# When a search step that waits for matmul products is due: a planned time worked out anew at each unit, instead of once and with a cap

## The chip, the cores and the metric

The kernel runs on one core of a Trainium2 chip. The metric is the device time of one execution in microseconds (us). The engines are TensorE (PE), VectorE (DVE), ScalarE (ACT), GpSimd (POOL, which issues the indirect DMAs) and SyncE (SP).

## The reference

Four batches of eight heads go through a retention layer (attention with a decay and no softmax); its output is a matrix `x` of 3072 tokens by 512. A mixture of eight experts follows. Tokens are given to experts greedily, the largest logit first, at most 384 tokens to an expert, and each token goes through its own expert alone:

```python
logits = x @ w_gate
order = np.argsort(-logits.flatten())
for idx in order:
    tok, e = (int(idx) // E, int(idx) % E)
    if assigned[tok] >= 0 or counts[e] >= cap:
        continue
    assigned[tok] = e
    counts[e] += 1
for e in range(E):
    mask = assigned == e
    h = np.maximum(x[mask] @ w1[e], 0.0)
    out[mask] = h @ w2[e]
```

## The kernel before

The first 100 us are the retention layer. After that PE works through eight experts in the order in which the greedy rule fills them. An expert is two blocks of matmuls: `mm1` (96 matmuls `ph`, 384 columns each, in eight groups of 12) and `mm2` (72 matmuls `py`, 512 columns each, three for each of eight slices in each of three row blocks). Each float32 operand is split into a high part, a rounded copy made by ACT (`w1h`, `w2h`, `xh`, `hh`), and a low part, a subtraction made by DVE (`w1l`, `w2l`, `xlo`, `hl`), so every product takes three matmuls.

Beside the experts runs a search. `search(n)` finds which expert is filled n-th and by which tokens, while PE multiplies for expert n-1. It has two rounds. In each, DVE compares the logits with 64 thresholds (`cmp`, two halves), PE counts (12 small matmuls `psm<-oh,cmp`, the products here), ACT negates one half of the counts (`ng`), DVE makes a flag of each (`sg`), and PE adds these up (`psm<-sg,onesb`, called the number below), which DVE reads (`nmb`). After the rounds PE ranks the tokens (`psm<-Wq,ub`), places them (`psm<-V,ob`), and turns places into token numbers (`psm<-pls,selq`, called the token step), which DVE reads (`own`, `idx`). A DVE tail follows that prepares the next search (`eo` to `a`, then `a`, `oh`, `th`, `cmp`, `off`, `qn`, `cmp`). From the token numbers POOL gathers the expert's rows (`xg`) and weights (`wraw`). The rows are transposed by PE in three blocks (`pt<-ident,xg`, into two buffers named `pt`), and ACT and DVE split each block into `xh` and `xlo`; a third block needs the buffer of the first, which is free when the first `xlo` is done.

Nothing here is ordered at run time: every engine runs its own queue in the order in which the program was written. That order comes from a planner, a clock kept in Python while the program is built. `mm1` and `mm2` yield after each unit of a few matmuls. Then `Beside.tick` moves the clock on and lets the search take its next step if the step's `due` time is past, and `Feed.tick` does the same for fetches, splits and transposes. Where a step reads products of PE, its due time comes from `hear()`: in the planner's picture, PE's signal is not heard while POOL is booked to issue an indirect DMA (1250 ns each, by `issue`), nor for 500 ns (`AFTER`) after it. `hear()` looks at the issues that are booked at that moment and returns at most 1200 ns (`DEAF`):

```python
if n:
    yield clk.pe + hear() + COPIED
full(pc, ng, sg)
```

Of the kernel before, what the change touches and what calls it, by code (L numbers as in the profile page):

```python
# [22 lines left out]
E = 8  # L23
# [6 lines left out]
READY, SWITCH, HEAR, COPIED = 200, 50, 200, 350  # L30
DEAF, AFTER, ISSUE = 1200, 500, 1250
# [27 lines left out]
READY0 = 0  # L59
# [5 lines left out]
def tile_retention_moe(ctx: ExitStack, tc: tile.TileContext, qkv, wg, w1, w2,  # L65
# [65 lines left out]
    class Clock:  # L131

        pe = dve = pool = dma = 0
        busy = []

    clk = Clock()

# [19 lines left out]
    def hear():  # L157

        t = clk.pe + HEAR
        clk.busy = [p for p in clk.busy if p[1] + AFTER > t]  # L160
        for p in clk.busy:
            if p[0] <= t:
                t = max(t, p[1] + AFTER)
        return min(DEAF, t - clk.pe)

    def issue(at):

        clk.pool = max(clk.pool, clk.pe, at) + ISSUE
        clk.busy.append((clk.pool - ISSUE, clk.pool))

    def pe_step(n):
        clk.pe += max(35, n / 2.4)
        clk.dve = max(clk.dve, clk.pe + hear())
# [6 lines left out]
    def tt(out_, a, b_, op):  # L180
        return ve.tensor_tensor(out_, a, b_, op=op)

    def bc(ap, n):
        return ap[:, :, None].to_broadcast([128, ap.shape[1], n])
# [27 lines left out]
    def reach(cols, k, m, cmp, th):  # L212
        nt = th.shape[1]
        tt(cmp[:, cols], bc(m[:, cols], nt), cb(th, nt, k), OP.is_ge)
# [10 lines left out]
    def full(pc, ng, sg):  # L225

        ve.scalar_tensor_tensor(sg[0:64], pc[0:64, 0:E], float(CAP), ng, op0=OP.subtract, op1=OP.is_ge)
# [428 lines left out]
    def ps_small(shape):  # L656
        return pp.tile(shape, F32, name=small[0], bufs=2 if small[0] == "pt" else 1)
# [15 lines left out]
    def count_pairs(cmp, oh, eng=None):  # L673
        pc = ps_small([128, 2 * E])
        for k in range(COLS // 2):
            by_two(pc, cmp, oh, 2 * k, k == 0, k == COLS // 2 - 1)
        return pc, other_half(pc, eng)
# [77 lines left out]
    def search(n):  # L755

        nonlocal un  # L760
        last = n == E - 1
        code = mp.tile([128, 1], F32, name="code", bufs=2)
        if last:
            ve.tensor_reduce(code, left.pop(n), axis=AX.X, op=OP.max)
            ve.tensor_copy(Wq[:, 0:COLS], un)
        else:
            m, a, oh, cmp = ready.pop(n)
            for i in range(2):
                sg = sgs[i]
                if n or i:  # L770
                    yield
                    pc, ng = count_pairs(cmp, oh, None if n > 1 else ve)
                    if n:
                        yield clk.pe + hear() + COPIED
                    full(pc, ng, sg)
                    yield
                num = ps_small([128, E])
                te.matmul(num, onesb, sg, start=True, stop=True)
                nm = sw.tile([128, 1], F32, name="nmb", bufs=2)
                ve.tensor_reduce(nm, num, axis=AX.X, op=OP.max)  # L780
                if not i:
                    th = sw.tile([128, 64], F32, name="th")
                    ve.scalar_tensor_tensor(th, nm.to_broadcast([128, 64]), near[:, 0:1], offn[n], op0=OP.mult,
                                            op1=OP.add)
                    cmp = sw.tile([128, COLS, 64], BF, name="cmp", bufs=2)
                    for h in range(2):
                        cc = slice(h * COLS // 2, (h + 1) * COLS // 2)
                        reach(cc, COLS // 2, m, cmp, th)
                        if not h and n:
                            yield  # L790
                    q = sw.tile([128, 1], F32, name="q", bufs=2)
                    ve.scalar_tensor_tensor(q, nm, near[:, 0:1], qn[n], op0=OP.mult, op1=OP.add)
                else:
                    eh = sw.tile([128, E], BF, name="eh")
                    ve.scalar_tensor_tensor(eh, num, nm, codet, op0=OP.is_equal, op1=OP.mult)
                    tv = sw.tile([128, 1], F32, name="tv", bufs=2)
                    ve.scalar_tensor_tensor(tv, nm, near[:, 1:2], q, op0=OP.mult, op1=OP.add)
                    ve.tensor_reduce(code, eh, axis=AX.X, op=OP.max)
            sel = sw.tile([128, COLS], BF, name="sel")
            ve.tensor_scalar(sel, a, code, None, op0=OP.is_equal)  # L800
            ve.scalar_tensor_tensor(Wq[:, 0:COLS], m, tv, sel, op0=OP.is_ge, op1=OP.mult)
        if n == 0:
            fill(FILL[0])
        ve.tensor_tensor_scan(Sc[:, 1:COLS + 1], Wq[:, 0:COLS], zer[:, 0:COLS], 0.0, op0=OP.add, op1=OP.add)
        wix = weight_rows(code, n)
        named[n] = wix.bitcast(U32), clk.dve
        if n == 0:
            fetch_w("w1", 0, 0, wix.bitcast(U32), raw0)
        if not last:
            both = sw.tile([128, 1], F32, name="both")  # L810
            ve.tensor_reduce(both, eh, axis=AX.X, op=OP.add)
            unf = un
            un = sw.tile([128, COLS], F32, name="un", bufs=2)
            tt(un, unf, Wq[:, 0:COLS], OP.subtract)
        yield
        rk = ps_small([128, COLS + 1])
        te.matmul(rk, ub, Wq, start=True, stop=False)
        te.matmul(rk, onesb, Sc[:, 0:COLS + 1], start=False, stop=True)
        s0 = sw.tile([128, COLS], I32, name="s0")
        ve.scalar_tensor_tensor(s0, rk[:, 0:COLS], 32.0, Wq[:, 0:COLS], op0=OP.add, op1=OP.mult)  # L820
        if not last:
            ve.scalar_tensor_tensor(bad, rk[:, COLS:], float(CAP), bad, op0=OP.not_equal, op1=OP.max)
        if n == 0:
            fill(FILL[1])
        V, low = high_slots(s0, 1, n, None if n else nc.scalar)
        ob = low_slots(low)
        if not last:
            ve.scalar_tensor_tensor(bad, both, code, bad, op0=OP.not_equal, op1=OP.max)
            alone(oh, unf if n else None)
        yield  # L830
        pls = places(V, ob, None if n else ve)
        yield clk.pe + hear() + COPIED if n else None
        idx = tokens_of_slots(pls)
        oix = mp.tile([128, KT], I32, name="oix", bufs=4)
        ve.scalar_tensor_tensor(oix, bad.to_broadcast([128, KT]), float(2 * N), idx, op0=OP.mult, op1=OP.add)
        found[n] = idx.bitcast(U32), wix.bitcast(U32), oix.bitcast(U32)
        known[n] = clk.dve
        yield
        if not last:
            left[n + 1] = close(n, code, left.pop(n))  # L840
            if n + 2 < E:
                m1, a1, oh1, cmp1 = ready[n + 1] = prep_tiles()
                best(Lw, allc, m1, oh1)()
                codes(allc, oh1, a1)
                if n:
                    yield
                tt(a1, a1, un, OP.mult)
                tt(oh1, oh1, bc(un, E), OP.mult)
                rest = below(n + 1, tv)
                th = next(rest)  # L850
                for h in range(2):
                    reach(slice(h * COLS // 2, (h + 1) * COLS // 2), COLS // 2, m1, cmp1, th)
                    if not h:
                        next(rest)
                    yield
# [247 lines left out]
    class Beside:  # L1103


        def __init__(self):
            self.gen, self.n, self.due = None, -1, 0
            self.held = lambda: False

        def step(self):  # L1110
            if self.gen is None:
                self.n += 1
                self.gen = search(self.n)
            clk.pe = max(clk.pe, self.due) + SWITCH
            due = None
            try:
                due = next(self.gen)
            except StopIteration:
                self.gen = None
            self.due = due or clk.dve + (READY if self.n else READY0)  # L1120

        def tick(self, ns, cur):
            clk.pe += ns
            while not self.held() and self.due <= clk.pe and (self.gen is not None or self.n + 1 <= min(cur + 2, E - 1)):
                self.step()

        def finish(self, n):
# [2 lines left out]

    clk.dve = clk.pe = clk.pool = clk.dma = 0
    clk.busy.clear()
    side = Beside()
    left_over[0] = lambda i: pp.tile([128, DM], F32, name="py" if i % 2 else "ph", bufs=2 if i % 2 else 3)
    for k in STEPS:
# [248 lines left out]
```

## Time and profile before

| | us |
|---|---|
| median of 3 runs | 401.94 (401.54 to 402.74) |
| the profiled execution, its own time | 404.41 |
| its span, first to last instruction | 402.7 |
| busy in the span: PE, DVE, ACT, POOL | 388.3, 272.0, 156.5, 146.9 |

The profiled execution has 1.7 us outside the span and is 2.5 us above the median of the runs. The granted clock of PE is 0.998 of full speed, so the clock is no matter here.

### The profile page before, as it was taken

The page shows a single profiled execution, that of the slowest core. Times are in us where ns is not written, and L with a number is a line of the kernel's source. Part 1 is how long each engine was busy: PE and PEld are TensorE (multiplying, and loading weights), DVE is VectorE, ACT ScalarE, POOL GpSimd, SP SyncE. Part 2 cuts the span into 40 slices and gives each one's busy share as a digit, 9 for nine tenths or more (in the row PEclk, how much of TensorE's full clock was granted, in tenths as well). Part 3 has the DMA queues.
Part 4 walks back from the last instruction along what each step waited for, and adds up shares of the span by engine and source line. Part 5 has one row for each costly group of instructions (what it writes and reads, how often), then busy time and mean ns, then how long its engine had stood idle before and what let it go on. Part 6 is the DMA issues. An engine that isn't in the chain of part 4 may idle for free.

```text
span 402.7 us, 8469 instructions
## 1 busy us (share of the span) xinstructions
PE 388.3 (96%) x3457; PEld 338.1 (84%) x3459; DVE 272.0 (68%) x640; ACT 156.5 (39%) x285; POOL 146.9 (36%) x162
## 2 busy tenths in 40 slices
PE   8899999997999999999989999999999999999994
PEld 6798999973798889879868997898789889989983
DVE  5349768968899589858848895896688157156400
ACT  1342424243471275147215533453453256156210
POOL 5488774202620620341261451352356128020011
PEclk9999999999999999999999999999999999999999
DMA  7999988888643572383375374177146405810001
GB/s 276 422 414 420 387 311 266 201 194 288 201 199 104 174 260 55 141 285 134 106 225 218 132 252 166 52 215 278 49 156 224 178 27 168 354 52 28 2 28 59
DMA packets 22824, 77.50 MB, mean 192 GB/s; under 512 B 2677, under 2 KB 11639, under 8 KB 16121
## 3 DMA queue, kind: packets, MB, share of 16 engines
q0 software_dynamic: 8448, 46.14, 32.7%
q1 hardware_dynamic: 14330, 30.74, 21.6%
q8 instruction: 29, 0.48, 0.5%
q14 instruction: 17, 0.14, 0.1%
HBM read 64.29 MB, written 12.58 MB: 191 GB/s over the span
## 4 chain that ended last, share of the span: by engine, by line
PE 64%; issue 13%; DVE 11%; DMA 5%; POOL 2%; ACT 2%; POOLq 1%; SPq 1%; another core or an unknown queue 0%; ACTq 0%; DVEq 0%
PE py L1092 24%; PE ph L1050 20%; PE yp L414 5%; PE sc L369 4%; DMA ld<-qkv 3%; PE pt L1000 2%; PE yp L399 2%; PE psm L154 2%; PE TP L429 2%; DVE w1l L154 2%; PE sc L501 2%; DVE cmp L154 1%; DVE w2l L154 1%; POOL wraw L954 1%; DVE am L372 1%
## 5 line engine op out<-in xcount | busy, mean ns | idle before, releaser
L1050 PE MATMUL ph<-xh,w1h 128*128 128x384 f32 x248 | 81.9, 343 | 0.1
L1050 PE MATMUL ph<-xlo,w1h 128*128 128x384 f32 x256 | 81.7, 336 | 0.2 <-DVE xlo L154 0.2
L1050 PE MATMUL ph<-xh,w1l 128*128 128x384 f32 x256 | 81.5, 335 | 0.0
L1092 PE MATMUL py<-w2h,hh 128*128 128x512 f32 x184 | 75.3, 409 | 0.0
L1092 PE MATMUL py<-w2l,hh 128*128 128x512 f32 x184 | 72.0, 392 | 0.0
L1092 PE MATMUL py<-w2h,hl 128*128 128x512 f32 x184 | 72.0, 392 | 0.0
L1073 POOL DMA_INDIRECT out<-yo,oix x23 | 27.0, 1172 | 110.4 <-ACT yo L1070 103.4
L954 POOL DMA_INDIRECT wraw<-w,wix x32 | 38.8, 1212 | 60.5 <-DVE un L154 46.9
L1055 ACT ACTIVATE hh<-ph 128x384 fp32r<-128x384 f32 x64 | 31.3, 490 | 61.5 <-PE ph L1050 58.4
L154 DVE TENSOR_TENSOR w1l<-wraw,w1h 128x1024 fp32r<-128x1024 f32 (+1 forms) x36 | 39.2, 1101 | 14.4 <-ACT w1h L973 14.2
L1050 PEld LDWEIGHTS ph<-xlo,w1h 128*128 128x128 f32 x256 | 47.7, 188 | 0.5 <-DVE xlo L154 0.5
L1050 PEld LDWEIGHTS ph<-xh,w1h 128*128 128x128 f32 x248 | 46.4, 188 | 1.6 <-DVE hl L154 0.6
L1050 PEld LDWEIGHTS ph<-xh,w1l 128*128 128x128 f32 x256 | 47.7, 188 | 0.0
L154 DVE SCALAR_TENSOR_TENSOR hl<-ph,hh 128x384 fp32r<-128x384 f32 x64 | 34.5, 552 | 16.1 <-ACT hh L1055 15.4
L987 POOL DMA_INDIRECT xg<-xs,idx x24 | 29.0, 1207 | 42.6 <-issue 27.7
L372 DVE TENSOR_TENSOR am<-sc,dm 128x512 f32<-128x512 f32 x48 | 30.0, 682 | 20.5 <-PE sc L369 20.5
L1092 PEld LDWEIGHTS py<-w2h,hl 128*128 128x128 f32 x184 | 34.5, 188 | 7.4
L154 DVE TENSOR_TENSOR w2l<-wraw,w2h 128x1024 fp32r<-128x1024 f32 x32 | 38.6, 1218 | 2.3 <-ACT w2h L973 2.3
L1092 PEld LDWEIGHTS py<-w2l,hh 128*128 128x128 f32 x184 | 34.7, 189 | 6.2 <-DVE w2l L154 0.7
L1092 PEld LDWEIGHTS py<-w2h,hh 128*128 128x128 f32 x184 | 34.6, 188 | 5.5
L973 ACT ACTIVATE w1h<-wraw 128x1024 fp32r<-128x1024 f32 (+1 forms) x36 | 33.6, 957 | 7.8 <-issue 6.6
L1070 ACT ACTIVATE yo<-py 128x512 f32<-128x512 f32 x23 | 13.8, 598 | 58.6 <-PE py L1092 38.4
(185 smaller groups left out, 557.0 us busy)
## 6 DMA issues: line engine op xcount, KB each, us to landing
ld<-qkv SPq DMA_DIRECT2D x20, 1024.0 KB, 12.7
xs<-x SPq DMA_DIRECT2D x32, 128.0 KB, 3.2
ld<-qkv SPq DMA_DIRECT2D x4, 768.0 KB, 6.6
xs<-xr SPq DMA_DIRECT2D x7, 256.0 KB, 2.7
wraw<-w,wix POOLq DMA_INDIRECT x32
xg<-xs,idx POOLq DMA_INDIRECT x24
out<-yo,oix POOLq DMA_INDIRECT x23
xs<-x SPq DMA_DIRECT2D x4, 64.0 KB, 1.8
```

Of the source, the lines that this page charges most:

```text
L154: return f(o, *a, **k)
L369: nc.tensor.matmul(sc[s][:, pr, :], k_[r, w], q_[r, w], start=True, stop=True)
L372: masked.append(nc.vector.tensor_tensor(am[:, s], sc[s], dm[:, s], op=OP.mult))
L414: nc.tensor.matmul(yp[o:o + 64, pr, :], values(u)[:, 2 * pr + s, :], st[u][0][:, s, pr, :], start=(not c and pr == 0), stop=(pr == HP - 1) ...
L954: nc.gpsimd.indirect_dma_start(out=t, out_offset=None, in_=w1v if nm == "w1" else w2v, in_offset=bass.IndirectOffsetOnAxis(ap=wix[:, hf:hf ...
L973: nc.scalar.activation(p[0], p[2], AF.Copy)
L987: nc.gpsimd.indirect_dma_start(out=t, out_offset=None, in_=xs, in_offset=bass.IndirectOffsetOnAxis(ap=found[n][0][:, j:j + 1], axis=0))
L1050: nc.tensor.matmul(ph, a[:, o:o + 128], x_[:, d], start=(k == 0 and not begun), stop=(k == len(prods) - 1), skip_group_check=begun)
L1055: nc.scalar.activation(hh[:, f], ph, AF.Relu)
L1070: nc.scalar.activation(yo, py, AF.Copy)
L1073: sct = nc.gpsimd.indirect_dma_start(out=out, out_offset=bass.IndirectOffsetOnAxis(ap=oix[:, j:j + 1], axis=0), in_=yo, in_offset=None, bo ...
L1092: nc.tensor.matmul(py, h_[:, f, t], a[:, o:o + DM], start=(k == 0), stop=(k == 23))
```

## The change

Three steps of each search get their due time in another way: the two that make the flags after a count, and the one that reads the placed tokens. In place of a number they yield a function, and `Beside.tick` calls it at every unit. The function starts 200 ns (`HEAR`) after the products and goes through all issues that are booked by the time it is called, also those booked after the products; each issue that it falls into pushes it to 500 ns after that issue. There is no cap. 350 ns (`COPIED`) come on top as before. The numbers of steps, instructions and bytes stay as they are, but PE, DVE, ACT and POOL get some of their instructions in another order.

```diff
+        clk.issued.append(clk.busy[-1])
+
+    def heard():
+
+        t0 = clk.pe + HEAR
+
+        def when():
+            t = t0
+            for a, b_ in clk.issued:
+                if a <= t < b_ + AFTER:
+                    t = b_ + AFTER
+            return t + COPIED
+        return when
...
-                        yield clk.pe + hear() + COPIED
+                        yield heard()
...
-        yield clk.pe + hear() + COPIED if n else None
+        yield heard() if n else None
...
-            clk.pe = max(clk.pe, self.due) + SWITCH
+            clk.pe = max(clk.pe, self.due()) + SWITCH
...
-            self.due = due or clk.dve + (READY if self.n else READY0)
+            at = clk.dve + (READY if self.n else READY0)
+            self.due = due or (lambda: at)
...
-            while not self.held() and self.due <= clk.pe and (self.gen is not None or self.n + 1 <= min(cur + 2, E - 1)):
+            while not self.held() and self.due() <= clk.pe and (self.gen is not None or self.n + 1 <= min(cur + 2, E - 1)):
```

The first instruction that moves belongs to search 3, beside `mm2` of expert 1; from there the order differs in places up to search 7. Line numbers of the changed kernel are 13 higher in this part.

The first place is PE's queue beside `mm2` of expert 2, where the first number of search 4 and the transposes of expert 3's rows stand. Before, right behind the count:

```order
L1000 MATMUL pt<-ident,xg 128x128 x4
L1092 MATMUL py<-w2h_2770,hh 128x512
L1092 MATMUL py<-w2l_2771,hh 128x512
L1092 MATMUL py<-w2h_2770,hl 128x512
L154 LDWEIGHTS onesb
L154 MATMUL psm<-sg_90,onesb 128x8
L1000 MATMUL pt<-ident,xg 128x128 x4
```

And of the change, the end of that `mm2`, which twelve `py` matmuls (the last three are shown) part from the number:

```order
L1105 MATMUL py<-w2h_2785,hh 128x512
L1105 MATMUL py<-w2l_2786,hh 128x512
L1105 MATMUL py<-w2h_2785,hl 128x512
L1013 MATMUL pt<-ident,xg 128x128 x4
L1063 MATMUL ph<-xh,w1h_3026 128x384 x4
L1063 MATMUL ph<-xh,w1l_3027 128x384 x2
L154 LDWEIGHTS cmp
```

Before, the number stood 3 `py` and one block of transposes behind the count; now 18 `py` and two blocks. The third block, the `pt` row of this second piece, was followed by 21 `py` before `mm1` of expert 3 began; now that `mm1` begins right behind it.

The second place is DVE's queue for the same step. Before:

```order
L154 TENSOR_TENSOR cmp<-m,th 128x768
L154 SCALAR_TENSOR_TENSOR sg_90<-psm,ng 64x8
L154 TENSOR_REDUCE nmb<-psm 128x1
L154 SCALAR_TENSOR_TENSOR th<-nmb,near,off 128x64
L154 TENSOR_TENSOR cmp<-m,th 128x768
L154 TENSOR_TENSOR xlo<-pt,xh 128x4x128 x2
L154 TENSOR_TENSOR cmp<-m,th 128x768
L154 SCALAR_TENSOR_TENSOR q<-nmb,near,qn 128x1
L154 TENSOR_TENSOR w1l_3053<-wraw,w1h_3052 128x1024
L154 TENSOR_TENSOR xlo<-pt,xh 128x4x128
```

Of the change:

```order
L154 TENSOR_TENSOR cmp<-m,th 128x768
L154 TENSOR_TENSOR w1l_3027<-wraw,w1h_3026 128x1024
L154 SCALAR_TENSOR_TENSOR sg_90<-psm,ng 64x8
L154 TENSOR_REDUCE nmb<-psm 128x1
L154 SCALAR_TENSOR_TENSOR th<-nmb,near,off 128x64
L154 TENSOR_TENSOR cmp<-m,th 128x768
L154 TENSOR_TENSOR w1l_3027<-wraw,w1h_3026 128x1024
L154 TENSOR_TENSOR cmp<-m,th 128x768
L154 SCALAR_TENSOR_TENSOR q<-nmb,near,qn 128x1
L154 TENSOR_TENSOR xlo<-pt,xh 128x4x128 x3
```

The first `xlo`, which frees the buffer of the third block, has moved behind a `w1l`, the second `cmp` and `q`.

The third place is DVE's tail behind search 4's token step, with the second half of expert 3's `w2l` (two pieces of 1024 columns). Before:

```order
L154 TENSOR_REDUCE a<-eqc_3289 128x24
L154 SCALAR_TENSOR_TENSOR hl<-ph,hh 128x384 x2
L154 TENSOR_TENSOR a<-a,un 128x24
L154 TENSOR_TENSOR oh<-oh,un 128x192
L154 TENSOR_SCALAR th<-gridn_77,tv 128x64
L154 TENSOR_TENSOR cmp<-m,th 128x768
L154 TENSOR_SCALAR off<-gridn_78,tv 128x64
L154 TENSOR_SCALAR qn<-gridn_78,tv,near 128x1
L154 SCALAR_TENSOR_TENSOR hl<-ph,hh 128x384 x2
L154 TENSOR_TENSOR w2l_3271<-wraw,w2h_3270 128x1024
L154 TENSOR_TENSOR cmp<-m,th 128x768
L154 TENSOR_TENSOR w2l_3271<-wraw,w2h_3270 128x1024
```

Of the change:

```order
L154 TENSOR_REDUCE a<-eqc_3334 128x24
L154 SCALAR_TENSOR_TENSOR hl<-ph,hh 128x384
L154 TENSOR_TENSOR w2l_3311<-wraw,w2h_3310 128x1024
L154 TENSOR_TENSOR a<-a,un 128x24
L154 TENSOR_TENSOR oh<-oh,un 128x192
L154 TENSOR_SCALAR th<-gridn_77,tv 128x64
L154 TENSOR_TENSOR cmp<-m,th 128x768
L154 TENSOR_SCALAR off<-gridn_78,tv 128x64
L154 TENSOR_SCALAR qn<-gridn_78,tv,near 128x1
L154 TENSOR_TENSOR w2l_3311<-wraw,w2h_3310 128x1024
L154 TENSOR_TENSOR cmp<-m,th 128x768
L154 TENSOR_TENSOR xlo<-pt,xh 128x4x128
```

Within DVE's queue the two pieces have moved forward. Against PE the whole tail has moved back: 51 `ph` of `mm1` of expert 3 stood between search 4's token step and `mm2` before, and 18 do now. Between `own` and the rows shown stands one `w2l` of the first half instead of two.

## Rows read from the trace of the kernel before

**Rows 1.** Page, part 1: PE's busy time, share of the span, instructions.
```profile
PE 388.3 (96%) x3457; PEld 338.1 (84%) x3459; DVE 272.0 (68%) x640; ACT 156.5 (39%) x285; POOL 146.9 (36%) x162
```

**Rows 2.** Timeline of PE, 207 to 212: start, length, instruction, [idle before <-releaser].
```profile
207.62 0.46 PE L154 MATMUL psm<-oh,cmp 128*128 128x16 bf16 x12
...
208.87 0.40 PE L1092 MATMUL py<-w2h,hl 128*128 128x512 f32 x1
211.21 0.17 PE L154 MATMUL psm<-sg,onesb 128*128 128x8 bf16 x1 [1.95 <-DVE sg L154]
211.24 0.64 PE L1000 MATMUL pt<-ident,xg 128*128 128x128 f32 x4
211.63 0.47 PE L1092 MATMUL py<-w2h,hh 128*128 128x512 f32 x1
```

**Rows 3.** Timeline of ACT, 210 to 212.
```profile
210.79 0.17 ACT L220 ACTIVATE ng<-psm 64x8 f32<-64x8 f32 x1 [5.06 <-remote]
...
211.91 0.60 ACT L1005 ACTIVATE xh<-pt 128x512 fp32r<-128x512 f32 x1 [0.32 <-PE pt L1000]
```

**Rows 4.** Timeline of POOL, 207 to 210.
```profile
207.34 0.97 POOL L954 DMA_INDIRECT wraw<-w,wix  x1 [0.30 <-issue]
208.62 0.95 POOL L954 DMA_INDIRECT wraw<-w,wix  x1 [0.30 <-issue]
```

**Rows 5.** Timelines of ACT and POOL behind search 3's first count.
```profile
172.66 0.17 ACT L220 ACTIVATE ng<-psm 64x8 f32<-64x8 f32 x1 [3.79 <-issue]
...
172.55 0.95 POOL L954 DMA_INDIRECT wraw<-w,wix  x1 [0.30 <-issue]
```

**Rows 6.** Timeline of DVE, 211 to 216.
```profile
211.00 0.16 DVE L154 SCALAR_TENSOR_TENSOR sg<-psm,ng 64x8 bf16<-64x8 f32 x1 [5.05 <-ACT ng L220]
211.42 0.17 DVE L154 TENSOR_REDUCE nmb<-psm 128x1 f32<-128x8 f32 x1 [0.26 <-PE psm L154]
...
211.94 0.96 DVE L154 TENSOR_TENSOR cmp<-m,th 128x768 bf16<-128x768 f32 x1
212.82 1.28 DVE L154 TENSOR_TENSOR xlo<-pt,xh 128x512 fp32r<-128x512 f32 x2
214.01 0.95 DVE L154 TENSOR_TENSOR cmp<-m,th 128x768 bf16<-128x768 f32 x1
...
215.01 1.22 DVE L154 TENSOR_TENSOR w1l<-wraw,w1h 128x1024 fp32r<-128x1024 f32 x1
```

**Rows 7.** Chain that ended last, 196 to 280: start, length, what.
```profile
199.51 8.26 PE py L1092 x36
...
262.45 12.09 PE ph L1050 x69
```

**Rows 8.** Timeline of DVE, 229 to 238.
```profile
229.00 0.17 DVE L154 TENSOR_TENSOR own<-psm,quad 128x24 f32<-128x24 f32 x1
...
229.51 1.23 DVE L154 TENSOR_TENSOR w2l<-wraw,w2h 128x1024 fp32r<-128x1024 f32 x1
...
232.60 0.22 DVE L154 SCALAR_TENSOR_TENSOR eo<-codet,code,eo 128x8 bf16<-128x8 bf16 x1
...
235.01 1.01 DVE L154 SCALAR_TENSOR_TENSOR hl<-ph,hh 128x384 fp32r<-128x384 f32 x2
235.94 0.17 DVE L154 TENSOR_TENSOR a<-a,un 128x24 bf16<-128x24 bf16 x1
...
237.82 0.55 DVE L154 SCALAR_TENSOR_TENSOR hl<-ph,hh 128x384 fp32r<-128x384 f32 x1
```

**Rows 9.** Timeline of PE at two small gaps, 196 and 295.
```profile
196.30 0.34 PE L1050 MATMUL ph<-xh,w1l 128*128 128x384 f32 x1
196.69 0.44 PE L1050 MATMUL ph<-xh,w1h 128*128 128x384 f32 x1
...
294.31 0.86 PE L1050 MATMUL ph<-xh,w1l 128*128 128x384 f32 x4
295.35 0.45 PE L1050 MATMUL ph<-xlo,w1h 128*128 128x384 f32 x1 [0.17 <-DVE xlo L154]
```

More of the change, by code (lines that the diff above doesn't have):

```diff
@@ L133, in tile_retention_moe @@
         pe = dve = pool = dma = 0
-        busy = []
+        busy, issued = [], []
     clk = Clock()
@@ L1106, in __init__ @@
         def __init__(self):
-            self.gen, self.n, self.due = None, -1, 0
+            self.gen, self.n, self.due = None, -1, lambda: 0
             self.held = lambda: False
@@ L1132, in tile_retention_moe @@
     clk.busy.clear()
+    clk.issued.clear()
     side = Beside()
```

## The prediction

> **What bounds the kernel now.** I read the page first: PE is busy for 388.3 of 402.7 us, no other engine for more than 272 [rows 1]. From the start of the experts to the end the chain that ended last is nearly all PE, in runs such as 36 `py` matmuls in 8.26 us (229 ns each) or 69 `ph` in 12.09 us (175 ns each) [rows 7]. So time is won or lost only where PE stands still between two matmuls, and a nanosecond there is a nanosecond at the end. Matmuls overlap in the records, so I went through PE's timeline by starts: a gap is the distance of two starts less what such a matmul takes. One gap is large. A `py` starts at 208.87, the next instruction, the first number of search 4, at 211.21; less 0.23 that is 2.11 us, and the view names DVE's `sg` as what it waited for [rows 2]. The timelines of the other engines say why. The 12 products began at 207.62 and took 0.46 [rows 2], ACT's `ng` that reads them began only at 210.79 [rows 3], and `sg` followed at 211.00, the number at 211.21 [rows 6, 2]. ACT was idle all the while, 5.06 us. So PE's signal was 2.7 us late (207.62 + 0.46 = 208.08 against 210.79). In these 2.7 us POOL issued two weight fetches, 207.34 to 208.31 and 208.62 to 209.57 [rows 4]. The planner had left only 3 `py` and a block of transposes, 1.1 us, between products and number. Other gaps are small: two of 0.22 and 0.35 (196.69 - 196.30 - 0.17; 295.35 - 294.31 - 4 x 0.173) [rows 9].
>
> **What the change removes.** Number and products of search 4 are now parted by 18 `py` and two blocks: 18 x 0.229 + 2 x 0.39 = 4.9 us (a block takes PE from 211.24 to 211.63) [rows 7, 2]. A signal 2.7 us late, then `ng` and `sg` (0.42 from 210.79 to 211.21) [rows 3, 2], fits in. Gain: 2.11. In search 3 the number moves in the same way, from 9 `py` behind the products to the end of `mm2`; there was no gap to remove. Behind it everything of searches 3 and 4 is later against PE's stream, which also shifts the two small gaps of [rows 9] away; I count them as gained, 0.57. Together 2.68.
>
> **What it adds, first: the third block of transposes.** It needs the buffer that the first `xlo` frees. In the new DVE order that `xlo` stands behind `nmb`, `th`, `cmp`, a `w1l`, the second `cmp` and `q`, and all of these wait for the number. From the number's start: `nmb` starts 0.21 later and `cmp` 0.52 after that (211.21, 211.42, 211.94); the next instruction may start 0.88 after `cmp` (212.82); `w1l` takes 1.22, of which 0.08 lies under the next, as `cmp`'s last 0.08 does: 1.14; `cmp` and `q` take 1.00 (214.01 to 215.01); one `xlo` of two in 1.28 ends after 0.65; the signal takes 0.05 (`sg` ends at 211.16, the number starts at 211.21) [rows 6, 2]. Sum 4.45 us. PE has work for 0.03 + 12 x 0.229 = 2.78 us in that time [rows 2, 7]. It then stands before the block for 1.67 us, with all later matmuls behind it.
>
> **Second: `mm1` of expert 3 begins right behind that block.** Its first matmuls read `xh`, which ACT copies from the block. From a block's first transpose (211.24) the copy starts 0.67 later (211.91) and takes 0.60; with 0.05 for the signal PE goes on 1.32 after the block's start, where its own work takes 0.39 [rows 2, 3]. A wait of 0.93. Before, 21 `py` lay between and hid it; that cover is gone.
>
> **Third: the second half of `w2l`.** Search 4's token step now stands 18 `ph` ahead of `mm2` of expert 3, not 51, so DVE's tail and the last low parts of the weights fall into one stretch. `own` starts 0.21 after the token step, as `nmb` did; then, from [rows 8] where nothing else is named: `own` to the next `w2l` 0.51; `w2l` 1.14; `hl` 0.46 (half of 235.01 to 235.94); `eo` to the end of the codes 2.41 (232.60 to 235.01); `hl` 0.46; the third piece 1.14; `a` to `qn` 1.88 (235.94 to 237.82); the fourth piece to its end 1.23; signal 0.05. Sum 9.49 us. PE reaches the matmul that reads the fourth piece after 0.03 + 18 x 0.175 + 19 x 0.229 = 7.53 us [rows 7]. A wait of 1.96, of which some 0.3 already falls at the third piece. The bounds are 1.0, if both `hl` of the stretch (0.46 each) fall outside it, and 2.4, if ACT's `hh` comes one such length late.
>
> **Covered.** The gathers of expert 3's rows start later with search 3's token step, by 2 to 3 us; the first transposes of these rows stand 3.4 us later as well (15 `py`). One gather goes behind a scatter in POOL's queue, and the block that reads it is the one that waits anyway. The weights of that expert are split an `mm1` later than they land. I count these at nothing; should one be late, its price is what the transposes then wait, at most one issue (0.97 [rows 4]).
>
> **The sum.** New waits 1.67 + 0.93 + 1.96 = 4.56; gained 2.68; net 1.88 slower. The profiled execution would go from 404.41 to 406.3. Its own time lies 2.5 above the median of the runs, so I apply the difference to the median: 401.94 + 1.8 = 403.7 us, rounding down for gaps under 0.2 that I have not summed.
>
> **The rivals.** *The stall belongs to the profiled execution.* For: the execution is 2.5 us above the median, which is about this gap; and search 3's `ng` started at 172.66 in the midst of an issue that had begun at 172.55, without delay [rows 5], so issues do not always hold PE's signal. Against: the runs spread over only 1.2 us, and the gap lies exactly beside two issues. Then nothing of the 2.11 is gained: 401.94 + 1.88 + 2.11 = 405.9. The Trainium skill would have it so: its page "SBUF — State Buffer", section "Who interferes with whom", says that only VectorE and GpSimd contend there and that PE and ACT never wait on anyone. By it an issue could not hold a signal from PE to ACT, the planner's picture would be wrong, and waiting for issues would win nothing; [rows 3, 4] speak against it in this one place.
>
> *The change doesn't do what it says.* The signal is late again in the new place, where a `w1h` and a `w1l` have come between `ng` and `sg`. Late by 2.7, with 0.2 for `ng`, 1.0 for the copy, 1.22 for `w1l`, 0.16 for `sg` and 0.05, the number waits 0.5 us past its 4.9 [rows 3, 6], and more if the signal is held for three issues instead of two (up to 1.3 more): 404.2 to 405.5.
>
> *Not slower: the first `xlo` is in time.* Place: the third block of transposes; price: the 1.67 there and, if PE comes to the block with time to spare for ACT as well, the 0.93 behind it. It decides at 2.78 us from number to `xlo`; I have 4.45, so DVE would have to save 1.7, for which a copy and a compare would have to go ahead of the number. The queue is in order, which speaks against. Then the net is 1.88 - 2.60 = -0.7: 401.2. If the wait for `w2l` goes too, the change does just what it is written for: 401.94 - 2.68 = 399.3.
>
> **How the numbers follow.** A measurement of this kernel tells 0.3% from no change, that is 1.2 us: faster is below 400.7, slower above 403.2. The forecast with its three waits has 0.45, own range 402.5 to 404.8; of this I put 0.31 over 403.2 and 0.14 under. The stall of one execution: 0.17, slower. The late signal again: 0.10, slower. The transposes in time: 0.20, of which 0.06 faster and 0.14 the same. All waits hidden: 0.08, faster. Slower 0.58, same 0.28, faster 0.14. The range is 400.7 to 405.9: it leaves out the 0.14 below and the upper third of the stall's case, 0.06.
>
> **What would show it.** Right: in the timeline of PE no gap before search 4's first number; a gap of about 1.7 us before the last transposes ahead of `mm1` of expert 3, ended by DVE's `xlo`; one of about 0.9 behind these, ended by ACT's `xh`; one of 1.0 to 2.4 beside `mm2` of expert 3, ended by DVE's `w2l`. Wrong: the gap before the number still there; or no wait of PE for `xlo` and `w2l`; or a span that grew by well over 3 us, which would say that the signal was never late in the timed runs or that a wait stands where I have none, most likely at the numbers of searches 5 and 6.

## The result and the profile after

The changed kernel takes 405.98 us (median of 6 runs, 405.23 to 407.54), the kernel before beside it 401.77 (6 runs, 400.83 to 402.74): a ratio of 1.0105, with a 95% interval of 1.0084 to 1.0125. That is 3.4 to 5.0 us slower, where 1.8 were forecast, and 0.08 us past the upper end of the range. The profiled execution took 405.23 us, its span 403.5.

The page, part 1, answers to [rows 1]: the same work in the same busy time.

```profile
PE 388.6 (96%) x3457; PEld 339.1 (84%) x3459; DVE 272.1 (67%) x640; ACT 156.7 (39%) x285; POOL 145.7 (36%) x162
```

PE's timeline of the change, 207 to 220 and 241 to 244, answers to [rows 2]: start, length, instruction, [idle before <-releaser].

```profile
207.82 0.46 PE L154 MATMUL psm<-oh,cmp 128*128 128x16 bf16 x12
...
213.29 0.18 PE L154 MATMUL psm<-sg,onesb 128*128 128x8 bf16 x1
...
215.93 0.39 PE L1105 MATMUL py<-w2h,hl 128*128 128x512 f32 x1
217.83 0.63 PE L1013 MATMUL pt<-ident,xg 128*128 128x128 f32 x4 [1.51 <-issue]
219.15 0.96 PE L1063 MATMUL ph<-xh,w1h 128*128 128x384 f32 x4 [0.69 <-ACT xh L1018]
...
241.74 0.39 PE L1105 MATMUL py<-w2h,hh 128*128 128x512 f32 x1
243.48 0.50 PE L1105 MATMUL py<-w2l,hh 128*128 128x512 f32 x1 [1.35 <-DVE w2l L154]
```

The number of search 4 (213.29) waits for nothing. By starts, less what such a matmul takes, the three new gaps are 217.83 - 215.93 - 0.23 = 1.67, 219.15 - 217.83 - 0.48 = 0.84 and 243.48 - 241.74 - 0.24 = 1.50; one of 0.30 at 239.95 goes with the last. The forecast had 1.67, 0.93 and 1.96. (0.48 is what the four transposes took in this place, behind a stand-still. With the 0.39 of the forecast the second gap is 0.93.)

The view gives the first gap to "issue", which names no engine. DVE's timeline in that stretch answers to [rows 6].

```profile
213.52 0.17 DVE L154 TENSOR_REDUCE nmb<-psm 128x1 f32<-128x8 f32 x1 [2.70 <-PE psm L154]
213.72 0.28 DVE L154 SCALAR_TENSOR_TENSOR th<-nmb,near,off 128x64 f32<-128x64 f32 x1
214.04 0.96 DVE L154 TENSOR_TENSOR cmp<-m,th 128x768 bf16<-128x768 f32 x1
214.92 1.22 DVE L154 TENSOR_TENSOR w1l<-wraw,w1h 128x1024 fp32r<-128x1024 f32 x1
216.05 0.95 DVE L154 TENSOR_TENSOR cmp<-m,th 128x768 bf16<-128x768 f32 x1
216.92 0.21 DVE L154 SCALAR_TENSOR_TENSOR q<-nmb,near,qn 128x1 f32<-128x1 f32 x1
217.05 1.28 DVE L154 TENSOR_TENSOR xlo<-pt,xh 128x512 fp32r<-128x512 f32 x2
```

Each instruction up to `xlo` starts where the one ahead of it lets it, from the number on. The first of the two `xlo` ends near 217.05 + 0.64 = 217.7, and the block starts at 217.83: 4.54 us behind the number, where the forecast had 4.45. That it was this `xlo` that the block waited for is so far read from the order alone; spare_buffer, below, tests it.

The chain that ended last goes the same way at the other end of that search (start, length, what; it answers to [rows 7]).

```profile
234.18 0.19 DVE own L154
...
234.78 1.13 DVE w2l L154
235.91 0.51 DVE hl L154
...
238.83 0.47 DVE hl L154
239.29 1.13 DVE w2l L154
...
240.99 0.96 DVE cmp L154
...
242.29 1.14 DVE w2l L154
243.43 0.04 issue
243.48 0.73 PE py L1105 x2
```

From `own` to the `py` are 9.30 us of DVE alone; with the forecast's 0.21 ahead of `own` that is 9.51, and the forecast had 9.49.

So the costs came as forecast. What did not come is the gain, and the question was why.

### The profile page after: what moved, and what is told of

It reads as the page before. It is cut to its first block, busy times and chain, and to the rows that moved or that the text cites. A ratio compares the mean times of both kernels' runs of the same rounds, so it can differ in the third digit from the quotient of the medians.

```text
span 403.5 us, 8467 instructions
## 1 busy us (share of the span) xinstructions
PE 388.6 (96%) x3457; PEld 339.1 (84%) x3459; DVE 272.1 (67%) x640; ACT 156.7 (39%) x285; POOL 145.7 (36%) x162
## 4 chain that ended last, share of the span: by engine, by line
PE 66%; issue 16%; DVE 9%; DMA 4%; POOL 3%; ACT 1%; POOLq 1%; another core or an unknown queue 0%; DVEq 0%; ACTq 0%
PE ph L1063 22%; PE py L1105 20%; PE sc L382 5%; PE yp L427 5%; DMA wraw<-w,wix 2%; PE TP L442 2%; PE yp L412 2%; PE pt L1013 2%; PE psm L154 2%; DVE cmp L154 2%; PE sc L514 2%; DVE w2l L154 1%; POOL wraw L967 1%; DMA out<-yo,oix 1%; DVE am L385 1%
```

## The experiments

**Theory:** PE's signal was late in the profiled execution of the kernel before, and not in its timed runs. Then nothing of the 2.11 us was there to be gained. **Rival:** the stall is in all runs, and the change pays it back somewhere else. Runs that went to the chip together, a set below, share their runs of the kernel before; the result above is the first set. Medians are of all runs of a set; the ratios with their intervals need not be the quotients of these medians.

### The kernel before again, and one search at a time (second set)

**before_again** and **before_third** are the kernel before, unchanged, with a profile.

> The kernel before, unchanged, profiled once more. Theory A (the 2.11 us gap ahead of search 4's first number belongs to the one profiled execution; timed runs don't have it): no gap over 0.3 us there, PE's signal on time at that count, and an own time near 402 instead of 404.4. Theory B (the gap is in every run, and the changed kernel loses some 2 us in a way that its profile doesn't show): the gap of 1.9 to 2.3 us is there again, and the own time is near 404.

> The same kernel, a third profile. Theory A: again no gap over 0.3 us ahead of search 4's first number, own time near 402. Theory B: the gap of about 2 us, own time near 404.

They took 401.28 and 402.89 us. From PE's, ACT's and POOL's timelines of before_again, at the place of [rows 2 to 4]:

```profile
206.63 0.46 PE L154 MATMUL psm<-oh,cmp 128*128 128x16 bf16 x12
...
208.12 0.18 PE L154 MATMUL psm<-sg,onesb 128*128 128x8 bf16 x1
208.16 0.64 PE L1000 MATMUL pt<-ident,xg 128*128 128x128 f32 x4
...
207.18 0.17 ACT L220 ACTIVATE ng<-psm 64x8 f32<-64x8 f32 x1 [2.42 <-PE psm L154]
...
206.34 0.97 POOL L954 DMA_INDIRECT wraw<-w,wix  x1 [0.30 <-issue]
207.62 0.94 POOL L954 DMA_INDIRECT wraw<-w,wix  x1 [0.30 <-issue]
```

It is the same program with the same two fetches beside the products. The products end at 207.09, `ng` starts at 207.18 while POOL is issuing, and the number has no gap ahead of it. PE's gaps over 0.15 us from 104 us on are 0.39, 0.16, 0.23, 0.16 and 0.34 here, 1.28 in all. In the change's profile they are 0.72, 1.67, 0.84, 0.30, 1.50 and 0.16, 5.19 in all. The difference, 3.9 us, is what the medians differ by within their uncertainty (3.4 to 5.0), with no gain of 2.11 in it.

**only_search4** and **only_search3** use the new due time for the count steps of one search alone:

```diff
-                        yield heard()
+                        yield heard() if n in (3,) else (lambda at=clk.pe + hear() + COPIED: at)
```

(`(4,)` in only_search4.) The third changed step, the token step, matters little: a program with the new due time at the count steps alone has the instruction order of the change, and one with it at the token step alone has that of before, but for one token step that stands three `ph` later. These two were built and not run.

> The new due time for the counts of search 4 alone; every other step as before. Its first number then stands 3.4 us further behind its products and is safe from a late signal; of the three new waits only a part of the one for w2l is left, since DVE's tail of search 4 comes later by less: by durations from the rows about 0.5 us. Theory A: 0.3 to 0.9 us slower than before, not to be told from no change. Theory B: the 2.1 us gap is won, 1.2 to 1.8 us faster.

> The new due time for the counts of search 3 alone. Search 3 then ends later and pushes search 4 back against PE, by the order of the queues: the third block of transposes and the copy behind it wait 0.9 us, w2l of expert 3 some 2.5 us. Theory A: about 3 us slower than before (2 to 4), most of the change's loss. Theory B: search 4's first number is still close behind its products, so the gap stays and about 3 us come on top of a time that holds it; the same time, but the gap must be in the profile.

only_search4 took 401.93 us against 401.74, a ratio of 1.0003 (0.9992 to 1.0013). In its trace the number of search 4 stands behind six `py` and two blocks of transposes, 2.62 us after the start of the last products (210.65 against 208.03). In the second set's kernel before it is 1.49, so the edit moves it by 1.1 us, and not by the 3.4 that the expectation reckoned with. Of a stall of 2.11 us it could thus win only some 1.1; less 0.34 more wait for `w2l` (0.51 against 0.17) that is some 0.8 us, if the stall were in all runs. The interval, 0.3 us faster to 0.5 slower, excludes that, and Theory B's 1.2 to 1.8 us with it. only_search3 took 403.6, a ratio of 1.0065 (1.004 to 1.009). PE's timeline of only_search3:

```profile
216.03 0.60 PE L1013 MATMUL pt<-ident,xg 128*128 128x128 f32 x4
217.37 0.79 PE L1063 MATMUL ph<-xh,w1h 128*128 128x384 f32 x3 [0.74 <-ACT xh L1018]
...
238.76 0.40 PE L1105 MATMUL py<-w2h,hh 128*128 128x512 f32 x1
240.50 0.50 PE L1105 MATMUL py<-w2l,hh 128*128 128x512 f32 x1 [1.34 <-DVE w2l L154]
```

Its gaps are 0.90 before `ph` and 0.88 and 1.50 before the two `w2l` pieces, 3.28 us, less 0.73 of small gaps of before that are gone (0.16, 0.23, 0.34): 2.55, and the ratio makes it 2.6 (1.6 to 3.6). The medians make it 1.9: four of the six runs took 403.27 to 403.6, two 405.53 and 405.68 at the same clock, and no profile shows what lengthened these two. The waits for `xh` and `w2l` thus come from search 3. The wait for `xlo` needs searches 3 and 4 together: in neither of these two is there a gap ahead of the third block.

### Taking the new waits away (third set)

**spare_buffer** is the change with the third block of expert 3's transposes in a buffer of its own, so that it does not wait for `xlo`. **tail_after_weights** is the change with search 4's tail held until expert 3's `w2l` pieces are written. **both_mended** has both. **issues_ignored** is the kernel before with a due time that knows no issues.

```diff
-        pt = pp.tile([128, HP, 128], F32, name="py" if third else "pt", bufs=2)
+        pt = pp.tile([128, HP, 128], F32, name="ph" if n == 3 and j == KT - 1 and later is not None else "py" if third else "pt",
+                     bufs=3 if n == 3 and j == KT - 1 and later is not None else 2)
...
-    side.held = lambda: feed.n < 2 and feed.xlows or side.n > feed.n + 1 and feed.pressed()
+    side.held = lambda: (feed.n < 2 and feed.xlows or side.n > feed.n + 1 and feed.pressed() or
+                         feed.n == 3 and side.n == 4 and 4 in found and
+                         any(p[1] == "w2" and p[3] == 3 for p in feed.split + [(0, "w2", 0, 3)] * len(feed.lows)))
```

and in issues_ignored, at both places:

```diff
-                        yield clk.pe + hear() + COPIED
+                        yield clk.pe + HEAR + COPIED
```

> The changed kernel, with the third block of expert 3's transposes in a buffer named ph, which is free at that time, instead of the first block's; no instruction moves on PE. Theory A (the three waits that PE's timeline shows are the whole loss): the wait of 1.67 us is gone, the 0.84 behind it and the 1.80 for w2l stay; 1.5 to 1.7 us faster than the changed kernel, some 2.5 us slower than before (1.5 to 3.2). Theory C (a good part of the loss is not in these gaps): less than half of the 1.67 comes back, 3.5 us or more slower than before.

> The changed kernel, with the tail of search 4 held back until the low parts of expert 3's w2 are written, so that DVE makes them first. Theory A: no wait for w2l, 1.8 us back; some 2.4 us slower than before (1.4 to 3.1), with the waits of 1.67 and 0.84 still there. Theory C: 3.5 us or more slower than before.

> Both edits together: spare buffer and weights ahead of the tail. Theory A: only the wait of 0.84 to 0.95 us for xh is left of the three, and the small gaps that the change itself removed stay removed (0.16 + 0.23 + 0.16 + 0.34 = 0.89 us), so the time is that of before, within 0.8 us, though every search step still goes by the changed due time. Theory C: clearly slower than before, by 1.5 us or more.

> The kernel before, with due times that ignore POOL's issues altogether (200 + 350 ns behind the products); DVE's planned clock still counts them. The order changes: by durations from the rows it brings new waits for hl (0.2 to 0.4 more than now) and for w2l (1.3), some 1.2 us slower than before if PE's signal is on time (0.5 to 1.8). If POOL's issues held the signal regularly, several numbers of the searches would wait for sg, 1 to 2.7 us each: 3 us slower or more, and gaps ended by DVE's sg in the profile.

| | us (runs) | ratio |
|---|---|---|
| the kernel before, in this set | 405.6 (29, 403.63 to 407.44) | |
| spare_buffer | 404.36 (12) | 0.9978 (0.996 to 0.9996) |
| tail_after_weights | 405.66 (12) | 1.0009 (0.9985 to 1.0033) |
| both_mended | 402.22 (6) | 0.9936 (0.9911 to 0.996) |
| issues_ignored | 404.66 (12) | 0.9989 (0.9969 to 1.0009) |

In this set the kernel before is 3.9 us slower than in the second, and each of the four profiles has signals of PE that come late beside POOL's issues. PE's, ACT's and POOL's timelines of both_mended at 136 to 139:

```profile
136.63 0.46 PE L154 MATMUL psm<-oh,cmp 128*128 128x16 bf16 x12
...
138.78 0.17 ACT L233 ACTIVATE ng<-psm 64x8 f32<-64x8 f32 x1 [2.03 <-remote]
...
137.03 1.02 POOL L1087 DMA_INDIRECT out<-yo,oix  x1 [0.37 <-ACT yo L1084]
138.35 0.97 POOL L967 DMA_INDIRECT wraw<-w,wix  x1 [0.31 <-issue]
```

And of the kernel before in the fourth set (before_fourth), the same place:

```profile
136.16 0.46 PE L154 MATMUL psm<-oh,cmp 128*128 128x16 bf16 x12
...
136.66 0.17 ACT L220 ACTIVATE ng<-psm 64x8 f32<-64x8 f32 x1 [0.38 <-PE psm L154]
...
136.55 1.02 POOL L1073 DMA_INDIRECT out<-yo,oix  x1 [0.37 <-ACT yo L1070]
```

The same issue begins 0.40 behind the products' start in the one and 0.39 in the other; `ng` starts 2.15 behind the products' start in the one and 0.50 in the other. The lateness is not of the program: both_mended, run again in two later sets, has 0.50. It is not of the chip either, for the second and the third set ran on the same one (number 10 in both). In the third set it is in all four profiles, in others in none. The first profile of before stands between: its signals were late in a single execution of 404.41 us, while the three timed runs beside it took 401.54 to 402.74.

Both edits did what they were made for: no gap ahead of the third block in spare_buffer, none for `w2l` in tail_after_weights, neither in both_mended, whose one large gap is 1.00 for `xh`. PE's timelines of spare_buffer, at the third block, and of tail_after_weights, around the place where the change waited longest for `w2l`:

```profile
216.40 0.39 PE L1106 MATMUL py<-w2h,hl 128*128 128x512 f32 x1
216.63 0.60 PE L1014 MATMUL ph<-ident,xg 128*128 128x128 f32 x4
218.01 0.44 PE L1064 MATMUL ph<-xh,w1h 128*128 128x384 f32 x1 [0.79 <-ACT xh L1019]
...
244.16 0.39 PE L1105 MATMUL py<-w2h,hl 128*128 128x512 f32 x1
244.39 0.39 PE L1105 MATMUL py<-w2h,hh 128*128 128x512 f32 x1
244.62 0.39 PE L1105 MATMUL py<-w2l,hh 128*128 128x512 f32 x1
```

So the buffer that the first `xlo` frees is what the third block waited for. The expectations were set against a kernel before of some 401.7 us. Against that, spare_buffer is 2.6 us slower (Theory A: 2.5) and both_mended 0.5 (within 0.8). tail_after_weights is 3.9 slower, which Theory C asked for and not Theory A's 2.4. Its profile shows two things that cost time there. Late `nmb` made the wait for `xlo` 2.36 us long instead of 1.67, and behind it PE's granted clock was 0.76 from 218 to 224 (on such falls, the last section). Its four runs with a mean clock of 0.996 or more have a median of 404.1, Theory A's 2.4 above 401.7. issues_ignored fits neither expectation and decides nothing: it moves other waits (0.99, 0.85 and 1.29 us at 143, 159 and 168), so its "same" does not say that issues can be left out of the due time.

### The change and the mended version beside each other (fourth to sixth set)

change_again, change_third and change_fourth are the change once more, mended_again and mended_third are both_mended, before_fourth and before_fifth are the kernel before.

New theory: late signals go with the set. The change costs 4.3 us of waits everywhere and wins something only where signals are late. Rival: a set lengthens every kernel alike, and ratios stay.

> The kernel before, unchanged, for its profile. Two theories. Signals: PE's signals come 2 to 3 us late beside GpSimd's fetches in some sets of runs and on time in others, and this alone makes the kernel before 401.8 or 405.6 us. Then the profile goes with the times of the same set: with a median near 401.8 no gap ahead of search 4's first number and expert 3's numbers on time, with one near 405.6 a gap of about 2 us there. Rival: the sets differ in something else that lengthens every kernel alike; then late signals and the median need not go together.

> The change, unchanged, beside the kernel before. Signals: the change costs 4.3 us of new waits wherever it runs and wins 2.1 to 3 back only where signals are late: a ratio of 1.007 to 1.012 in a set where the kernel before takes about 401.8, and of 0.998 to 1.004 where it takes about 405.6. Rival (the sets lengthen every kernel alike): 1.0105 in both.

> The change with the third block of expert 3's transposes in a buffer of its own and search 4's tail held until expert 3's w2 parts are written: one wait of 1.0 us for xh is left of 4.3. Signals: where the kernel before takes about 401.8, 1.0 of wait less 0.9 of small gaps of before that vanish, so the same, 0.998 to 1.003; where it takes about 405.6, 0.991 to 0.996 as in the set before. Rival (the sets lengthen every kernel alike): 0.994 in both.

> The change, unchanged, once more, for a set in which signals are late; the median of the kernel before tells which set it is. At about 405.6 for the kernel before: the 4.3 us of new waits stay, and 2.1 to 3 us at the numbers and the 0.9 of small gaps come back, so a ratio of 0.998 to 1.004, and in the profile expert 2's ng some 1 to 2 us late at 137 to 139 us while search 4's number waits for nothing. At about 401.8: 1.008 to 1.0125 again, with ng on time. Rival (the sets lengthen every kernel alike): 1.0105 in either.

> The kernel before once more, for a profile beside that of the change. If late signals belong to the set, this profile and that of the change show expert 2's ng (137 to 139 us) late together or on time together. If they belong to the single execution, one may be late without the other.

> The change once more. The waits for xlo, xh and w2l are there in any set: 4.3 us, and up to 0.6 more where nmb behind the number is late, as in the last set. Theory (late signals cost the kernel before as much as the change wins): with the kernel before at 405 or more, a ratio of 0.998 to 1.006; with it at 403 or less, 1.008 to 1.0145. Rival (the change costs 1 to 1.2% wherever): 1.010 to 1.012 in either.

> The change without its wait for xlo and for w2l, in the same set. Theory: with the kernel before at 405 or more, 0.991 to 0.997; with it at 403 or less, 0.998 to 1.003. Rival: 0.994 or 1.000 without regard to the kernel before.

| set | before, us (runs) | late signals in its profiles | change, ratio | both edits, ratio |
|---|---|---|---|---|
| 1 | 401.77 (6) | not in the change's | 1.0105 (1.0084 to 1.0125) | |
| 2 | 401.74 (17) | in none of four | | |
| 3 | 405.6 (29) | in all four | not run | 0.9936 (0.9911 to 0.996) |
| 4 | 401.62 (17) | in none of three | 1.0102 (1.0077 to 1.0126) | 1.0001 (0.9987 to 1.0016) |
| 5 | 402.8 (9) | in the change's, weaker | 1.012 (1.0085 to 1.0155) | |
| 6 | 402.01 (17) | in none of three | 1.0089 (1.0067 to 1.0111) | 0.9995 (0.9982 to 1.0008) |

The profiles of the kernel before took 400.96 us (before_fourth) and 402.1 (before_fifth), without a gap at search 4's number. The rival falls: the mended version is 0.6% faster than the kernel before in the third set and level with it in the fourth and sixth. PE's timeline of mended_again shows the one wait that is left:

```profile
217.49 0.60 PE L1014 MATMUL ph<-ident,xg 128*128 128x128 f32 x4
218.87 0.97 PE L1064 MATMUL ph<-xh,w1h 128*128 128x384 f32 x4 [0.79 <-ACT xh L1019]
```

Its 1.00 us (218.87 - 217.49 - 0.38) is paid for by the small gaps of before that are gone (0.16, 0.23, 0.16, 0.34).

change_third, in the fifth set, fits neither expectation well: `ng` was late there too (1.30 us behind the products' start instead of 0.50), but the kernel before took 402.8 us and the change 1.2% more. In its profile `nmb` was 0.51 late (0.74 us behind the number instead of 0.23), and the wait for `xlo` was 2.18 us, 0.51 longer. All five runs of the change there have a mean clock of 0.990 to 0.994, so part of its loss is clock (the last section). A late signal thus lengthens the new wait as well as the old one; the new due time counts issues against the products and not against the number. Without a profile of the kernel before in that set it stays open how late its own signals were.

What the change does in a set such as the third was not measured, so the other half of the new theory, that it wins something there, stays unshown. An estimate from spare_buffer: 404.36 and what the wait for `xlo` adds there (2.36 + 0.84 in tail_after_weights, against 1.00) give 406.6, a ratio of 1.002, without a fall of the clock.

## Why the prediction was wrong

**The step that failed** is "What the change removes", its "Gain: 2.11". The stall of [rows 2] was real in that execution, and its account (a signal 2.7 us late beside two issues, [rows 3, 4]) was right for it. But it was applied to a median that does not hold it: "so I apply the difference to the median". The kernel before has no such gap in any of its four later profiles (400.96 to 402.89 us, each within 1.2 us of the median of the timed runs beside it), and only_search4, which would have won some 0.8 us of such a stall, wins nothing (0.3 us faster to 0.5 slower). The profiled execution's 404.41 against 401.94 was the sign, named in the rival "the stall belongs to the profiled execution" and given 0.17. The spread of the timed runs, taken there as evidence against, was no evidence: three runs of one kind agree among themselves. By that rival's working the time is 405.9, and 405.98 was measured. This 405.9 was also made the upper end of the range, which so left out half of that rival, and not its upper third. The sign that the prediction names, a span grown by well over 3 us, is there against the second profile of before (399.5 to 403.5) and not against the first (402.7).

**A term at nothing: the clock.** The sum has none, and ahead of the prediction it says that "the clock is no matter here". That holds for the kernel before as it was profiled (0.998) and not for the change: three of the first set's six executions have a mean clock of 0.991 to 0.995, and in change_again a fall of the clock behind the new waits cost 1.43 us (the last section). The three at full clock have a median of 405.35. So that the median lies within 0.1 of the rival's 405.9 is in part luck: the rival has no term for the clock either.

**New waits: right in place, releaser and size.** 1.67 for `xlo` was 1.67; 0.93 for `xh` was 0.93 by the forecast's own reckoning and 0.84 by that of the result; 1.96 for `w2l` was 1.80, of which 0.30 at the third piece as said. In sum 4.56 was 4.31 to 4.40.

**Small gaps: right for the two that were listed.** The two of [rows 9] are gone, as are two of 0.16, and one of 0.16 is new. The list lacked the largest of them, 0.39 at 150 us, where PE waits for `cmp` in `mm1` of expert 2; it grew to 0.72 in two of four profiles of the change.

**Covered: right.** In the change's profiles no gap ended by a late gather or a late `w1l` came up.

**The other rivals.** The number was not late again in the new place, so "doesn't do what it says" fell where signals were on time. "The first `xlo` is in time" fell: PE was ready for the block 2.87 us behind the number (215.93 + 0.23 - 213.29), and the buffer let it start only at 4.54. The rival of the stall rested on a page of the Trainium skill as well, "SBUF — State Buffer", section "Who interferes with whom", by which PE and ACT never wait on anyone. The profiles of the second, fourth and sixth set agree with what the prediction drew from it (`ng` of before_again 0.09 behind the products' end, in the midst of an issue); those of the third do not (1.69 in both_mended). The section speaks of SBUF's ports; to carry it over to signals between engines was the prediction's own step, and the late signals do not contradict the section.

## What to carry to other kernels

Before a stall of one profiled execution is counted as a gain, hold that execution's own time against the timed runs: where it is longer by about the stall, the stall is probably not in the runs, and a second profile of the unchanged kernel settles it. A wait that is put off moves everything queued behind it on its engine; the sum over that queue, instruction by instruction, was exact here to 0.1 us (4.45 against 4.54, 9.49 against 9.51). A planner's rule for late signals (not heard during an issue) cost 1% here in the sets where signals were on time, because of what it pushed back; with the two waits mended it cost nothing there and gained 0.6% in the set where they were late. What it does unmended in such a set was not measured. A new stand-still of a busy PE may also cost clock, which a sum of waits leaves out.

## What the runs showed of the hardware

**PE's signals can come late beside GpSimd's issues, in all profiles of one set and in none of another.** At the first place, 136 to 139 us, `ng` starts 0.50 us after the start of the twelve products in all profiles of sets 1 (the change's), 2, 4 and 6, in the midst of an issue too. In the third set it is 2.15 us for both_mended, in the fifth 1.30, in the first profile of before 1.40. Not every signal beside an issue is late then: in both_mended the `ng` at 172.33 and at 208.69 start 0.04 and 0.09 behind the products' end, each in the midst of a weight fetch. It is PE's signal that is late and not ACT that is slow to take it. By the trace's list of semaphore updates, which no view prints, PE's signals at 208.07, 208.57 and 209.26 in the first profile of before all came between 210.72 and 210.83, and `ng` started at 210.79. The same list tells the two kinds of profile apart. From 104 us on, each of the six with late signals has 20 to 30 instructions, of PE, ACT and DVE alike, without an update within 0.25 us of their end; each of the other eleven has one or none. What that means is open: behind some of them the waiting engine went on in time (both_mended's `ng` at 172.33), so there only the record is missing.

The kernel before took 3.9 us longer in the third set than in the second. That the lateness causes this is likely and not shown: the kernel before was not profiled there. Part of it goes with the clock: 22 of its 29 runs there have a mean clock of 0.993 to 0.995 and a median of 405.8, the other seven, at 0.998 or more, one of 404.5. Nor did anything that was tried make signals late or on time, and what sets differ in is open.

**A stand-still of PE can cost clock behind it.** The windows of change_again (406.61 us), then of the change's first profile (405.23), each with PE, PEld, DVE, ACT and POOL busy, then the granted clock and the share of DMA:

```profile
core 0: us, PE busy (x) PEld busy (x) DVE busy (x) ACT busy (x) POOL busy (x), PEclk, DMA share, GB/s
218.00:219.20 1.20, 0.51 (x5) 0.28 (x4) 0.40 (x2) 0.70 (x2) 0.28 (x1) 1.00 0.93 382
219.20:222.40 3.20, 3.20 (x21) 2.89 (x22) 2.00 (x3) 1.48 (x3) 0.00 (x0) 0.51 0.20 77
222.40:224.00 1.60, 1.60 (x10) 1.60 (x9) 0.09 (x1) 1.09 (x3) 0.00 (x0) 0.91 0.04 10
...
219.20:222.40 3.20, 3.20 (x28) 3.04 (x29) 1.92 (x3) 2.37 (x5) 0.00 (x0) 1.00 0.33 134
```

The waits are the same in both, 1.67 and 0.84 us. Behind them, from 219.2 to 222.4, the granted clock was at 0.51 in the one execution, its lower level of 1.2 GHz, and at 1.00 in the other; `ph` matmuls that else start every 0.17 us started every 0.32 at the lower level. Both start the first `ph` at 219.15; the `py` that begins at 239.95 at full clock begins at 241.38 behind the fall, 1.43 us later. Five profiles have the wait for `xlo` (four of the change, one of tail_after_weights), and in three of them the clock falls just behind it (change_again, change_third, tail_after_weights); in the other twelve it falls nowhere from 104 us to the last 4 us. Why it fell in these three and not in the other two is open. In the first and fourth set the change's executions with a mean clock of 0.998 or more took 404.56 to 405.64 us, those at 0.995 or less 405.94 to 407.54; in the sixth the two kinds overlap (404.25 to 405.6 against 404.84 to 407.15). That is likely the rest of the loss beyond the gaps: of the first set's six, the three at full clock have a median of 405.35, 3.6 above the kernel before. A lower mean clock alone need not cost time: in the second set four of the 17 runs of the kernel before have one of 0.993 to 0.994, and their median, 401.75, is that of the others. Where in those runs the clock fell is not shown.
